# A threshold attention with two feed-forward layers: converted weights kept in memory, the conversion in wide operations on VectorE

## The chip, the core and the metric

One core of one Trainium2 chip. The metric is the device time of one execution in microseconds (us). Before the change three runs took 1331.09, 1331.42 and 1332.36 us; the median is 1331.42.

The engines in the profile: PE (TensorE, matmuls), PEld (its weight loads), DVE (VectorE), ACT (ScalarE), POOL (GpSimd), SP (SyncE, which here issues nearly all transfers on one queue, in program order).

## The reference

The inputs q, k, v have the shape (4, 8, 576, 64): 4 batches, 8 heads, 576 positions, 64 channels. The weights are 64-bit floating-point numbers, the other inputs 32-bit.

```python
scores = q @ k.T / sqrt(64)
keep   = scores >= rowmax(scores) - tau
attn   = softmax over the kept scores
x      = (attn @ v) -> 2304 tokens x 512
h      = sigmoid(x @ w_gate) * (x @ w_val)       # 512 -> 1536
x      = h @ w_out                               # 1536 -> 512
h2     = x @ w2_in                               # 512 -> 2048
g      = h2 if h2 >= 1, 0 if h2 <= -1, else (h2 + 1)**2 / 4
out    = g @ w2_out                              # 2048 -> 512
```

## The kernel before

The kernel sees a weight as a pair of 32-bit words and does no 64-bit arithmetic: each block of 512 columns (128 rows of a layer's weight block) is converted to 32 bit in parts. ScalarE takes the high word and scales it (`convert_a`, L139); VectorE clamps it (L153), shifts it left by three bits (L156), puts the sign in (L159), masks out the power of two (L164), multiplies that by the scaled low word (L169, two operations of 256 columns), and the two parts are added (L175, on GpSimd or VectorE). These are six kinds of operation, 512 columns each.

For precision every matmul operand is split into a rounded high part and the rest. A weight block becomes `ih`/`il` (for the first product) and `oh`/`ol` (for the second): ScalarE writes the high part (L191), the difference is a subtraction (L193, GpSimd). The hidden activations are split in the same way into `hh` (ScalarE, L707) and `hl` (GpSimd, L708). Each product is then three matmuls: high by high, high by low, low by high.

The work has three stages. Attention runs first (the function `attention`, up to about 400 us); in its background the first six blocks are converted into `keep0`. Then `ffn` runs layer 1 and layer 2. A layer goes over the 2304 tokens in three passes of 768 (`NPASS`), and a pass goes over the hidden features in blocks of 128: 12 steps a pass in layer 1, 16 in layer 2. The steps are numbered through here: layer 1 is steps 0 to 11, 12 to 23 and 24 to 35; layer 2 has 48 steps.

In a step of layer 1 TensorE computes, for each half of 384 tokens (n = 0, 1), the gate and the value (`up`, L654 to L656, 12 matmuls each) and then the second product of the step before (`down`, L744). The gate goes through a sigmoid on ScalarE (L692), VectorE multiplies it by the value (L696). The value lies in one PSUM buffer, so TensorE can begin the value of the next half only when VectorE has done this product. In a step of layer 2 VectorE clamps (L700), ScalarE squares (L703) and VectorE takes a maximum (L704).

All converted weights of a layer stay on the chip, in `keep0` and `w32`: layer 1 converts its remaining 30 blocks in the steps of its first pass (three a step, `parts_of`, L783), and in its last pass it converts the 32 blocks of layer 2 over them. The passes between convert nothing. The function `convert` (L658) asks for the raw words of the block three places ahead (`load_w`, L106: two transfers of 256 KB).

The order is written out by hand: each engine executes its instructions in the order in which the code calls them, and a call waits for its operands. At the end of a pass the next pass's tokens are split (`split_xs`, L638: four pieces on ScalarE and four subtractions on VectorE, L646, for each half). The row sums of the last attention pair go through memory: `drain` writes them (rs), `denom` (L461) inverts them and writes dr, `spread` (L469) broadcasts dr into a tile, and `normalise` (L476) multiplies on VectorE.

Of the kernel before, what the change touches and what calls it, by code (L numbers as in the profile page):

```python
# [23 lines left out]
def f32(ap):  # L24

    return ap.bitcast(F32)
# [3 lines left out]
def kernel(  # L30
# [37 lines left out]
    stage = ctx.enter_context(pool("stage", 6))  # L68
    raw = ctx.enter_context(pool("raw", 2))
    zero = ctx.enter_context(pool("zero", 1, space=DRAM))  # L70
    cv = ctx.enter_context(pool("cv", 1))
# [11 lines left out]
    keep0 = const.tile([P, 6 * KD * P], F32, name="keep0")  # L83
# [4 lines left out]
    third = cv.tile([P, 2, KD * P], F32, name="third")  # L88
    raws, wsp, pools, wsp_n = {}, {}, {}, []
    keep, spares = [], []  # L90
# [12 lines left out]
    def nat_tile():  # L103
        return stage.tile([P, S], F32, tag="nat", name="nat")

    def load_w(ph, g):  # L106

        f, i = divmod(g, 3 - ph)
        ins, wo = ((w_gate, w_val), w_out) if ph == 0 else ((w2_in,), w2_out)
        if i < len(ins):  # L110
            src = ins[i][:, 2 * f * P : 2 * (f + 1) * P].rearrange("(k p) f -> p k f", p=P)
        else:
            src = wo[f * P : (f + 1) * P, :].rearrange("p (k f) -> p k f", k=KD)
        hk = KD // 2
        for h in range(2):
            early = ph == 0 and g < 6
            t = raw.tile([P, KD * P], F32, tag="raw", name="raw") if early else nat_tile()[:, : KD * P]
            r = t.bitcast(U32)
            nc.sync.dma_start(
                out=r.rearrange("p (k f) -> p k f", k=hk), in_=src[:, h * hk : (h + 1) * hk]  # L120
            )
            raws[ph, g, h] = r.rearrange("p (f w) -> p f w", w=2)

    def part(g):
        at, o = (keep0, g) if g < 6 else (keep[0], g - 6)
        return at[:, o * KD * P : (o + 1) * KD * P]

    def slot(ph, g):

        n = g % 3  # L130
        if ph == 0 and g < 15:
            n = 2 if g < 6 else (1, 2, 1)[g % 3]
        if n == 2:
            return third[:, 0], third[:, 1]
        if n == 1 and not spares:
            spares.append(raw.tile([P, KD * P], F32, tag="raw", name="raw"))
        return (spares[0] if n else f32(his[0][:, : KD * P])), f32(both[:, n, : KD * P])

    def convert_a(ph, g):  # L139
        c, _ = slot(ph, g)  # L140
        hw = KD * P // 2
        for h in range(2):
            nc.scalar.activation(
                c[:, h * hw : (h + 1) * hw], raws[ph, g, h][:, :, 1].bitcast(F32), AF.Copy, scale=2.0**-112
            )

    def convert_b(ph, gs):


        at = {g: slot(ph, g) for g in gs}  # L150
        hw = KD * P // 2
        for c, a in at.values():
            nc.vector.tensor_scalar(c, c, -DBL_TOP, DBL_TOP, op0=ALU.max, op1=ALU.min)  # L153
            yield
        for c, a in at.values():
            nc.vector.tensor_scalar(a.bitcast(U32), c.bitcast(U32), 3, None, op0=ALU.logical_shift_left)  # L156
            yield
        for c, a in at.values():
            nc.vector.scalar_tensor_tensor(  # L159
                a.bitcast(U32), c.bitcast(U32), 0x80000000, a.bitcast(U32), op0=ALU.bitwise_and, op1=ALU.bitwise_or  # L160
            )
            yield
        for c, a in at.values():
            nc.vector.tensor_scalar(c.bitcast(U32), a.bitcast(U32), 0xFF800000, None, op0=ALU.bitwise_and)  # L164
            yield
        for h in range(2):
            for g, (c, a) in at.items():
                ch = c[:, h * hw : (h + 1) * hw]
                nc.vector.scalar_tensor_tensor(  # L169
                    ch, raws.pop((ph, g, h))[:, :, 0], 2.0**-52, ch, op0=ALU.mult, op1=ALU.mult  # L170
                )
                yield
        for g, (c, a) in at.items():
# [3 lines left out]
    def split_parts(ph, t, f, eng):  # L177
# [10 lines left out]
        for i in range(ni + 1):  # L188
            w = part(f * (ni + 1) + i)
            hi, lo = (oh, ol) if i == ni else (x[:, i].rearrange("p k f -> p (k f)") for x in (ih, il))  # L190
            nc.scalar.activation(hi, w, AF.Copy)  # L191
            yield
            eng.tensor_tensor(lo, w, f32(hi), op=ALU.subtract)  # L193
            yield

    def attention():
# [9 lines left out]
        qk = sb1("qk", 1)  # L206
        per, vp, pe_, pp, ph, sm, tp, rp = (
# [276 lines left out]
        def background():  # L484

            for g in range(6):
# [3 lines left out]
                convert_a(0, g)  # L490
                yield
                yield from convert_b(0, (g,))
# [47 lines left out]
        first = split_parts(0, 0, 0, nc.vector)  # L540
        for t, i in sched:
# [51 lines left out]
            if on:  # L593
# [18 lines left out]
                if t == N - 2:  # L612
                    for g in range(6, 9):
                        load_w(0, g)
# [16 lines left out]
    def ffn(att):  # L631


        with ExitStack() as st:
# [23 lines left out]
            def convert(ph, gs):  # L658
                run(convert_b(ph, gs))
                for g in gs:  # L660
                    i = fresh.index((ph, g)) + 3
                    if i < len(fresh):
                        load_w(*fresh[i])

            def hidden(ph, t, f, parts, after, nxt):
# [4 lines left out]
                ready = (ph, t, f, 0) in early  # L670
                lone = ph == 0 and t == 0
# [217 lines left out]
```

## Time and profile before

| | |
|---|---|
| runs | 1331.09, 1331.42, 1332.36 us |
| profiled execution | 1331.3 us, of which 1329.5 us is the span of its instructions |
| PE busy | 1230.3 us (93%) |
| DVE busy | 809.5 us (61%) |
| POOL busy | 775.6 us (58%) |
| ACT busy | 605.7 us (46%) |
| mean granted TensorE clock | 0.972 of full speed |
| moved by DMA | 87.66 MB |

The shares are averages over stages that differ. The stages are read one by one: attention up to about 400 us, layer 1's pass with a conversion (406 to 587), its pass without (587 to 740), its last pass, which converts for layer 2 (740 to 922), and layer 2 (922 to the end). A busy time of an engine means that an instruction is being executed or held on it; a matmul's end is modelled.

### The profile page before, as it was taken

To read this page: it belongs to the slowest core of one execution; us is meant where nothing else is said; L and a number is where in the kernel's file an instruction comes from. 1 tells how busy PE (TensorE), PEld (TensorE's weight loads), DVE (VectorE), ACT (ScalarE), POOL (GpSimd) and SP (SyncE) were. 2 spreads that over 40 slices of the span, in tenths; PEclk is the share of its full clock that TensorE was granted. 3 is DMA by queue.
4 is the path that set the end of the run, shared out by engine and by line. 5 is a ranking of instruction groups with operands and counts; after the bars stand their busy time and mean duration, and the time that the engine had idled before them with its cause. 6 is when DMAs were issued, how large, how long until landed. Compare 5 with 4: busy or idle time off the path is not lost.

```text
span 1329.5 us, 18928 instructions
## 1 busy us (share of the span) xinstructions
PE 1230.3 (93%) x6904; PEld 1127.6 (85%) x6904; DVE 809.5 (61%) x1148; ACT 605.7 (46%) x1240; POOL 775.6 (58%) x655
## 2 busy tenths in 40 slices
PE   7998999898988888899999888899999999999998
PEld 7887878787887777789999888789999899989997
DVE  6787987977877999951001999996222422243222
ACT  4666666665772333342223433334333533344333
POOL 6576777776774555555344556555555555555553
PEclk8999998998989999999999998989999999999999
DMA  4646565554212332310000233320000000001001
GB/s 139 156 125 158 123 156 138 130 151 120 70 60 69 101 100 96 95 32 1 0 1 0 64 96 103 114 85 1 1 0 1 19 30 1 0 1 48 0 1 48
DMA packets 61921, 87.66 MB, mean 66 GB/s; under 512 B 10832, under 2 KB 33313, under 8 KB 61828
## 3 DMA queue, kind: packets, MB, share of 16 engines
q1 hardware_dynamic: 61684, 86.46, 23.0%
q8 instruction: 54, 0.88, 0.3%
q14 instruction: 39, 0.32, 0.1%
q10 hardware_dynamic: 144, 0.00, 0.0%
HBM read 54.77 MB, written 4.81 MB: 45 GB/s over the span
## 4 chain that ended last, share of the span: by engine, by line
PE 44%; DVE 21%; issue 3%; DMA 2%; ACT 2%; POOL 0%; DVEq 0%; SPq 0%; ACTq 0%; POOLq 0%
PE w L752 14%; PE pu L654 5%; PE pu L655 5%; PE pu L656 5%; PE w L744 5%; DVE both L159 4%; PE pgv L654 3%; PE pgv L656 3%; PE pgv L655 3%; DVE both L156 2%; DVE third L156 2%; DVE act L696 2%; DVE raw L153 2%; DVE third L159 1%; DVE raw L169 1%
## 5 line engine op out<-in xcount | busy, mean ns | idle before, releaser
L708 POOL TENSOR_TENSOR hl<-act,hh 128x384 fp32r<-128x384 f32 x168 | 175.3, 1043 | 331.4 <-ACT hh L707 320.9
L414 POOL TENSOR_TENSOR plo<-p,phi 128x576 fp32r<-128x576 f32 x144 | 209.0, 1452 | 101.5 <-ACT phi L413 95.1
L654 PE MATMUL pgv<-xflat,ih 128*128 128x384 f32 x560 | 197.8, 353 | 50.2 <-DVE act L696 36.3
L707 ACT ACTIVATE hh<-act 128x384 fp32r<-128x384 f32 x168 | 88.2, 525 | 270.9 <-DVE act L696 209.2
L656 PE MATMUL pgv<-xflat,il 128*128 128x384 f32 x560 | 192.6, 344 | 0.0
L655 PE MATMUL pgv<-xflat,ih 128*128 128x384 f32 x560 | 192.3, 343 | 0.0
L654 PEld LDWEIGHTS pgv<-xflat,ih 128*128 128x128 f32 x560 | 108.5, 194 | 67.6 <-DVE act L696 46.2
L700 DVE TENSOR_SCALAR act<-pu 128x384 f32<-128x384 f32 x96 | 53.5, 557 | 174.7 <-PE pu L656 174.7
L193 POOL TENSOR_TENSOR il<-w,ih 128x512 fp32r<-128x512 f32 x99 | 134.7, 1368 | 7.4 <-ACT ih L191 7.4
L703 ACT ACTIVATE act<-act,half 128x384 f32<-128x384 f32 x96 | 58.5, 610 | 172.7 <-DVE act L700 172.7
L406 DVE SCALAR_TENSOR_TENSOR p<-w,cthr,ex 128x576 f32<-128x576 f32 x144 | 116.4, 808 | 30.3 <-ACT ex L400 28.1
L654 PE MATMUL pu<-xflat,ih 128*128 128x384 f32 x384 | 129.7, 338 | 2.2 <-DVE act L704 2.2
L400 ACT ACTIVATE ex<-w 128x576 f32<-128x576 f32 x144 | 93.6, 650 | 81.4 <-PE w L330 39.4
L655 PE MATMUL pu<-xflat,ih 128*128 128x384 f32 x384 | 129.4, 337 | 0.1
L656 PE MATMUL pu<-xflat,il 128*128 128x384 f32 x384 | 129.2, 336 | 0.0
L696 DVE TENSOR_TENSOR act<-pgv,act 128x384 f32<-128x384 f32 x70 | 38.6, 552 | 133.2 <-PE pgv L656 133.2
L356 DVE TENSOR_REDUCE mx<-w 128x1 f32<-128x576 f32 x144 | 107.6, 748 | 17.0 <-PE w L384 11.1
L752 PE MATMUL w<-oh,hh 128*128 128x512 f32 x288 | 113.0, 393 | 0.0
L752 PE MATMUL w<-oh,hl 128*128 128x512 f32 x288 | 112.8, 392 | 0.0
L752 PE MATMUL w<-ol,hh 128*128 128x512 f32 x288 | 112.8, 392 | 0.0
L704 DVE TENSOR_TENSOR act<-pu,act 128x384 f32<-128x384 f32 x96 | 53.5, 557 | 95.2 <-ACT act L703 95.2
L655 PEld LDWEIGHTS pgv<-xflat,ih 128*128 128x128 f32 x560 | 108.7, 194 | 1.1
(159 smaller groups left out, 3102.3 us busy)
## 6 DMA issues: line engine op xcount, KB each, us to landing
nat<-in_moe_w_out_dram SPq DMA_DIRECT2D x52, 256.0 KB
nat<-in_moe_w_in_dram SPq DMA_DIRECT2D x32, 256.0 KB
k<-hi_k SPq DMA_DIRECT2D x50, 144.0 KB
xflat<-hi_q SPq DMA_DIRECT2D x20, 288.0 KB
nat<-in_moe_w_gate_dram SPq DMA_DIRECT2D x20, 256.0 KB
nat<-in_moe_w_val_dram SPq DMA_DIRECT2D x20, 256.0 KB
nat<-in_v_dram SPq DMA_DIRECT2D x16, 288.0 KB
out_dram<-xall SPq DMA_DIRECT2D x17, 256.0 KB
```

The source lines that it names most:

```text
L193: eng.tensor_tensor(lo, w, f32(hi), op=ALU.subtract)
L356: nc.vector.reduce_max(mxs[p % 2][:, u : u + 1], w[:, :, :HS], axis=AX.XY)
L400: nc.scalar.activation(ex, dt[p, u][:, :, :HS], AF.Exp, scale=float(D) ** -0.5)
L406: nc.vector.scalar_tensor_tensor(pr, w[:, :, :HS], cthr, ex, op0=ALU.is_ge, op1=ALU.mult)
L414: nc.gpsimd.tensor_tensor(lo, pr, f32(hi), op=ALU.subtract)
L654: nc.tensor.matmul(ps, ih[:, i, kk], xh[:, kk, c], start=(kk == 0), stop=False)
L655: nc.tensor.matmul(ps, ih[:, i, kk], xl[:, kk, c], start=False, stop=False)
L656: nc.tensor.matmul(ps, il[:, i, kk], xh[:, kk, c], start=False, stop=(kk == KD - 1))
L707: nc.scalar.activation(hh[:, c], act, AF.Copy)
L708: nc.gpsimd.tensor_tensor(hl_[:, c], act, f32(hh[:, c]), op=ALU.subtract)
L744: nc.tensor.matmul(at(y, a, b), l[:, ds_], r[:, c], start=new and m == 0, stop=last and m == 2, skip_group_check=True,)
L752: nc.tensor.matmul(y[i % 3][:, i // 3], l[:, ts_], r, start=first and m == 0, stop=last and m == 2,)
```

## The change

No weights stay on the chip. A group of blocks is now one step's weights: three blocks (1536 columns) in layer 1, two (1024 columns) in layer 2. The clamp, the shift, the sign, the mask and the addition run once for a whole group; the multiplication by the low words stays one operation for each block, of 512 columns now. The result goes into one of five tiles (`ring`) or one of two (`w2s`), and from there to a tensor in the chip's memory (`saved`). Each step of the later passes fetches its weights from there two steps ahead (`load_step`). The groups of layer 2 are converted from step 10 on, five operations a step, over the second and the third pass of layer 1. In layers 1 and 2 every subtraction and addition that GpSimd had is VectorE's, the subtraction for `il` in one operation of 1024 columns in layer 1. GpSimd has no work there any more; its rows go from 494 to 247 in the whole program. Raw words arrive in transfers of 512 KB instead of 256 KB.

The core of the diff:

```diff
     def load_w(ph, g):
-        hk = KD // 2
-        for h in range(2):
-            early = ph == 0 and g < 6
-            t = raw.tile([P, KD * P], F32, tag="raw", name="raw") if early else nat_tile()[:, : KD * P]
+        early = ph == 0 and g < 6
+        t = (raw if early else pools["words"]).tile([P, 2 * KD * P], F32, tag="raw", name="raw")
+        r = t.bitcast(U32)
+        nc.sync.dma_start(out=r.rearrange("p (k f) -> p k f", k=KD), in_=src)
...
+    def load_step(ph, t, f):
+        w32[ph, t, f] = turn()
+        nc.sync.dma_start(out=w32[ph, t, f][:, : (3 - ph) * KD * P], in_=saved[ph, f])
+
+    def extract(ph, gs, c):
+        n = KD * P
+        for i, g in enumerate(gs):
+            nc.scalar.activation(
+                c[:, i * n : (i + 1) * n], raws[ph, g][:, :, 1].bitcast(F32), AF.Copy, scale=2.0**-112
             )
...
+    def convert(ph, gs, c, a):
+        n = KD * P
+        c, a = c[:, : len(gs) * n], a[:, : len(gs) * n]
+        cu, au = c.bitcast(U32), a.bitcast(U32)
+        nc.vector.tensor_scalar(c, c, -DBL_TOP, DBL_TOP, op0=ALU.max, op1=ALU.min)
+        yield
+        nc.vector.tensor_scalar(au, cu, 3, None, op0=ALU.logical_shift_left)
+        yield
+        nc.vector.scalar_tensor_tensor(au, cu, 0x80000000, au, op0=ALU.bitwise_and, op1=ALU.bitwise_or)
+        yield
+        nc.vector.tensor_scalar(cu, au, 0xFF800000, None, op0=ALU.bitwise_and)
+        yield
+        for i, g in enumerate(gs):
+            ci = c[:, i * n : (i + 1) * n]
             nc.vector.scalar_tensor_tensor(
+                ci, raws.pop((ph, g))[:, :, 0], 2.0**-52, ci, op0=ALU.mult, op1=ALU.mult
             )
             yield
-            eng = nc.vector if g % 3 == 2 else nc.gpsimd
-            eng.tensor_tensor(part(g), a, c, op=ALU.add)
+        nc.vector.tensor_tensor(a, a, c, op=ALU.add)
+        yield
...
+            def conversions():
+                for j, (ph, f, gs) in enumerate(todo):
+                    if j == 0:
+                        extract(ph, gs, highs[0])
+                    dst = turn() if ph == 0 else w2s[j % 2]
+                    if ph == 0:
+                        w32[0, 0, f] = dst
+                    ops = convert(ph, gs, highs[j % 2], dst)
+                    for m, _ in enumerate(ops):
+                        if m == 3 + len(gs):
+                            for g in todo[j + 2][2] if j + 2 < len(todo) else ():
+                                load_w(todo[j + 2][0], g)
+                        if m < 4 + len(gs):
+                            yield
+                    nc.sync.dma_start(out=saved[ph, f], in_=dst[:, : len(gs) * KD * P])
+                    if j + 1 < len(todo):
+                        extract(*todo[j + 1][::2], highs[(j + 1) % 2])
+                    yield
...
-                    nc.gpsimd.tensor_tensor(hl_[:, c], act, f32(hh[:, c]), op=ALU.subtract)
...
+                    run(itertools.islice(sp, 1) if n == 0 else itertools.islice(work, 1))
+                    nc.vector.tensor_tensor(hl_[:, c], act, f32(hh[:, c]), op=ALU.subtract)
+                    run(sp)
                     if n == 0 and nxt and nxt[2] == 0:
                         xs = split_xs(*nxt[:2], HT, T)
                         run(split_xs(*nxt[:2], 0, HT))
+                    run(itertools.islice(work, 2) if n == 0 else work)
                 run(xs)
...
+            todo = [(0, f, range(3 * f, 3 * f + 3)) for f in range(2, NF[0])]
+            todo += [(1, f, range(2 * f, 2 * f + 2)) for f in range(NF[1])]
...
                 if free:
+                    pools["words"] = sb("words", 6)
+                    for _, _, gs in todo[:2]:
+                        for g in gs:
+                            load_w(0, g)
...
+            for f in range(2):
+                nc.sync.dma_start(out=saved[0, f], in_=w32[0, 0, f])
...
             for s in range(len(order)):
                 nxt = order[s + 1] if s + 1 < len(order) else None
-                hidden(*order[s], parts_of(s), parts_of(s + 1), nxt)
+                t = order[s][:2]
+                ops = 8 if t == (0, 0) else 5
+                if s + 2 < len(order) and order[s + 2][:2] > (0, 0):
+                    load_step(*order[s + 2])
+                hidden(*order[s], nxt, itertools.islice(conv, ops))
```

How the change moves VectorE's instructions in a step of layer 1's first pass is shown by two pieces of its order. Before, from one product L696 of step 1 to the next, with the conversions of two blocks between them (`third`, `raw`, `both`: the working tiles; `nat`: the raw words; `w`: the kept weights):

```order
L696 TENSOR_TENSOR act<-pgv,act 128x384
L153 TENSOR_SCALAR third<-third 128x512
L156 TENSOR_SCALAR third<-third 128x512
L159 SCALAR_TENSOR_TENSOR third<-third 128x512
L164 TENSOR_SCALAR third<-third 128x512
L169 SCALAR_TENSOR_TENSOR third<-nat,third 128x256 x2
L153 TENSOR_SCALAR raw<-raw 128x512
L156 TENSOR_SCALAR both<-raw 128x512
L159 SCALAR_TENSOR_TENSOR both<-raw,both 128x512
L164 TENSOR_SCALAR raw<-both 128x512
L169 SCALAR_TENSOR_TENSOR raw<-nat,raw 128x256 x2
L175 TENSOR_TENSOR w_4793<-both,raw 128x512
```

Now, the whole of step 2 on VectorE (line numbers of the changed kernel; L689 is the product, L702 `hl`, L183 `il` and `ol`; `high` and `w` are the working tile and the converted weights):

```order
L689 TENSOR_TENSOR act<-pgv,act 128x384
L183 TENSOR_TENSOR il<-w_3_4804,ih 128x1024
L702 TENSOR_TENSOR hl<-act,hh 128x384
L183 TENSOR_TENSOR ol<-w_3_4804,oh 128x512
L147 TENSOR_SCALAR high_4801<-high_4801 128x1536
L149 TENSOR_SCALAR w_4_4805<-high_4801 128x1536
L689 TENSOR_TENSOR act<-pgv,act 128x384
L151 SCALAR_TENSOR_TENSOR w_4_4805<-high_4801,w_4_4805 128x1536
L702 TENSOR_TENSOR hl<-act,hh 128x384
L153 TENSOR_SCALAR high_4801<-w_4_4805 128x1536
L157 SCALAR_TENSOR_TENSOR high_4801<-raw,high_4801 128x512 x3
L161 TENSOR_TENSOR w_4_4805<-w_4_4805,high_4801 128x1536
```

The four subtractions that were GpSimd's stand among VectorE's instructions now, the conversion is spread over both halves of the step, and what the next step splits (`w_4_4805`) is written by the step's last instruction.

The transfers on SP's queue at the end of attention, before (`rs`, `dr` and `both` are the last pair's row sums on their way; `nat` receives raw words):

```order
L473 DMA rb<-dr 128x1x576
L459 DMA rs<-hi_q 64x1x9
L459 DMA rs<-sums 64x1x9
L119 DMA nat<-in_moe_w_gate_dram 128x2x256 x2
L466 DMA dr<-rs 128x9
L473 DMA both<-dr 128x1x576
```

And now (L121 `load_w`, L801 and L663 the stores of converted weights, L450 `drain`, L457 `denom`, L464 `spread`):

```order
L464 DMA rb<-dr 128x1x576
L450 DMA rs<-hi_q 64x1x9
L121 DMA raw<-in_moe_w_gate_dram 128x4x256
L121 DMA raw<-in_moe_w_val_dram 128x4x256
L121 DMA raw<-in_moe_w_out_dram 128x1024
...
L450 DMA rs<-sums 64x1x9
L801 DMA saved_0_89<-w_0_82 128x1536
L801 DMA saved_1_90<-w_1_83 128x1536
...
L663 DMA saved_2_91<-w_2_4803 128x1536
L457 DMA dr<-rs 128x9
L464 DMA both<-dr 128x1x576
```

Six transfers of raw words stand ahead of the last row sums, and two stores, three more transfers of raw words and a third store ahead of the row sums' way back to the chip. In code order the third of those stores and `denom` follow step 0's whole conversion.

## Rows read from the trace of the kernel before

**Rows 1.** Windows: busy time of each engine by stage; the first row names the columns.

```profile
core 0: us, PE busy (x) PEld busy (x) DVE busy (x) ACT busy (x) POOL busy (x), PEclk, DMA share, GB/s
0.00:400.00 400.00, 356.89 (x2316) 326.51 (x2317) 321.95 (x424) 260.35 (x522) 281.09 (x246) 0.94 0.49 127
...
406.00:587.00 181.00, 152.24 (x820) 135.36 (x820) 165.93 (x227) 63.74 (x149) 102.39 (x77) 1.00 0.28 89
587.00:740.00 153.00, 152.83 (x875) 146.19 (x873) 25.31 (x44) 49.02 (x103) 70.02 (x61) 1.00 0.00 1
740.00:922.00 182.00, 161.70 (x851) 151.70 (x852) 169.22 (x233) 66.29 (x153) 106.47 (x81) 0.93 0.26 84
922.00:1329.50 407.50, 401.60 (x2019) 363.31 (x2017) 125.19 (x221) 166.33 (x314) 214.22 (x190) 1.00 0.03 12
```

**Rows 2.** Timeline of VectorE (start us, us, instruction): steps 0, 12, 24; layer 2.

```profile
406.25 0.56 DVE L696 TENSOR_TENSOR act<-w,act 128x384 f32<-128x384 f32 x1
...
586.68 0.56 DVE L696 TENSOR_TENSOR act<-pgv,act 128x384 f32<-128x384 f32 x1 [2.38 <-PE pgv L656]
...
739.30 0.55 DVE L696 TENSOR_TENSOR act<-pgv,act 128x384 f32<-128x384 f32 x1
...
921.75 0.56 DVE L704 TENSOR_TENSOR act<-pu,act 128x384 f32<-128x384 f32 x1 [0.69 <-ACT act L703]
```

**Rows 3.** Timeline of VectorE inside step 1, one conversion.

```profile
418.54 0.41 DVE L153 TENSOR_SCALAR raw<-raw 128x512 f32<-128x512 f32 x1
418.99 1.39 DVE L156 TENSOR_SCALAR both<-raw 128x512 uint32<-128x512 uint32 x1
420.42 0.69 DVE L159 SCALAR_TENSOR_TENSOR both<-raw,both 128x512 uint32<-128x512 uint32 x1
...
422.56 0.76 DVE L169 SCALAR_TENSOR_TENSOR raw<-nat,raw 128x256 f32<-128x256 uint32 x2
423.36 0.69 DVE L175 TENSOR_TENSOR w<-both,raw 128x512 f32<-128x512 f32 x1
```

**Rows 4.** Timeline of GpSimd (POOL), the instruction beside them.

```profile
418.70 1.40 POOL L175 TENSOR_TENSOR w<-third 128x512 f32<-128x512 f32 x1 [0.70 <-DVE third L169]
```

**Rows 5.** Timeline of VectorE: first products of steps 13 and 23.

```profile
599.25 0.56 DVE L696 TENSOR_TENSOR act<-pgv,act 128x384 f32<-128x384 f32 x1 [3.45 <-PE pgv L656]
...
725.16 0.56 DVE L696 TENSOR_TENSOR act<-pgv,act 128x384 f32<-128x384 f32 x1 [7.87 <-PE pgv L656]
```

**Rows 6.** Instructions of L646: durations min/median/max, first and last start.

```profile
L646 DVE TENSOR_TENSOR xflat<-xall,xflat x44: 541/548/1652, 354.9 to 1190.7; 128x384 fp32r<-128x384 f32 x40, 128x768 fp32r<-128x768 f32 x4
```

**Rows 7.** Timeline of VectorE: other widths, alone.

```profile
17.79 0.45 DVE L273 CAST hi_k<-nat 128x576 fp32r<-128x576 f32 x1
...
425.04 0.76 DVE L480 TENSOR_TENSOR xall<-hi_q,both 128x576 f32<-128x576 f32 x1 [0.52 <-DMA both<-dr]
```

**Rows 8.** Timeline of ScalarE (ACT): two widths.

```profile
379.18 0.84 ACT L644 ACTIVATE xflat<-xall 128x768 fp32r<-128x768 f32 x1
...
415.35 0.62 ACT L191 ACTIVATE ih<-w 128x512 fp32r<-128x512 f32 x1
```

**Rows 9.** Chain of waits into the layers: start, us, what.

```profile
396.14 7.84 DMA rs<-hi_q
...
413.52 2.80 DMA dr<-rs
...
416.34 8.68 DMA both<-dr
```

**Rows 10.** Windows of 1 us: the last two columns are DMA share and GB/s.

```profile
401.00:402.00 1.00, 1.00 (x9) 1.00 (x8) 0.00 (x0) 0.00 (x0) 0.00 (x0) 1.00 0.13 51
...
414.00:415.00 1.00, 1.00 (x7) 1.00 (x7) 0.94 (x2) 0.74 (x3) 0.22 (x1) 1.00 0.99 333
...
1063.00:1064.00 1.00, 1.00 (x8) 1.00 (x7) 0.13 (x1) 0.17 (x1) 0.13 (x1) 1.00 1.02 391
```

**Rows 11.** Timeline of VectorE at a layer-2 pass end.

```profile
1049.50 3.85 DVE L646 TENSOR_TENSOR xflat<-xall,xflat 128x384 fp32r<-128x384 f32 x4 [2.11 <-ACT xflat L644]
```

More of the change, by code (lines that the diff above doesn't have):

```diff
@@ L86 @@
     both = const.tile([P, 2, S], F32R, name="both")
-    third = cv.tile([P, 2, KD * P], F32, name="third")
-    raws, wsp, pools, wsp_n = {}, {}, {}, []
-    keep, spares = [], []
+    raws, wsp, pools, wsp_n, highs, stages = {}, {}, {}, [], {}, []
+    w32 = {(0, 0, 0): ring[0], (0, 0, 1): ring[1]}
+    saved = {
+        (ph, f): scratch.tile([P, (3 - ph) * KD * P], F32, name=f"saved{ph}_{f}")
+        for ph in range(2) for f in range(NF[ph])
+    }
     wides = [ps_w.tile([P, 2, 512], F32, name=f"w{i}") for i in range(3)]
@@ L124, in part @@
[L124 to L137, printed above, removed]
@@ L187, in split_parts @@
         wsp[ph, t, f] = (ih, il, oh, ol)
-        for i in range(ni + 1):
-            w = part(f * (ni + 1) + i)
-            hi, lo = (oh, ol) if i == ni else (x[:, i].rearrange("p k f -> p (k f)") for x in (ih, il))
+        n = KD * P
+        fh, fl = (x.rearrange("p i k f -> p (i k f)") for x in (ih, il))
+        steps = [(0, ni)] if whole else [(i, i + 1) for i in range(ni)]
+        at = [(fh[:, i * n : j * n], fl[:, i * n : j * n], i, j) for i, j in steps] + [(oh, ol, ni, ni + 1)]
+        for hi, lo, i, j in at:
+            w = w32[ph, t, f][:, i * n : j * n]
             nc.scalar.activation(hi, w, AF.Copy)
             yield
-            eng.tensor_tensor(lo, w, f32(hi), op=ALU.subtract)
+            nc.vector.tensor_tensor(lo, w, f32(hi), op=ALU.subtract)
             yield
@@ L206, in attention @@
         qk = sb1("qk", 1)
+        stages.append(sb1("stage", 6))
         per, vp, pe_, pp, ph, sm, tp, rp = (
@@ L656, in up, with hidden @@
                     nc.tensor.matmul(ps, il[:, i, kk], xh[:, kk, c], start=False, stop=(kk == KD - 1))
[L658 to L665, printed above, removed]
+            def conversions():
[16 more added lines that the diff above has]
+                    yield
+            def hidden(ph, t, f, nxt, work):
                 hh = hs.tile([P, T], F32R, tag="hh", name="hh")
                 hl_ = hs.tile([P, T], F32R, tag="hl", name="hl")
-                ready = (ph, t, f, 0) in early
-                lone = ph == 0 and t == 0
-                if len(parts) > 2 or parts and not lone:
-                    for p in parts[1:2]:
-                        convert_a(*p)
-                    convert(parts[0][0], [parts[0][1]])
-                    parts = parts[1:]
-                if nxt and nxt not in wsp:
-                    sp = split_parts(*nxt, nc.gpsimd)
-                else:
-                    sp = iter(())
+                sp = split_parts(*nxt) if nxt and nxt not in wsp else iter(())
                 xs = iter(())
@@ L693, in hidden @@
                             up(0, t, f, n, 1, pv)
-                        for p in () if ready else parts[1:] if n == 0 else after[:1]:
-                            convert_a(*p)
+                        if n == 0:
+                            run(itertools.islice(sp, 1))
                         nc.vector.tensor_tensor(act, pv, act, op=ALU.mult)
@@ L720, in hidden @@
                         run(split_xs(*nxt[:2], 0, HT))
+                    run(itertools.islice(work, 2) if n == 0 else work)
                 run(xs)
-                if ready:
-                    for p in parts + after[:1]:
-                        convert_a(*p)
-                    convert(ph, [g for _, g in parts])
-                run(sp)
                 hts[ph, t, f] = (hh, hl_)
@@ L804, in ffn @@
             more = first_up()
[L805 removed]
+            second = split_parts(0, 0, 1, False)
             for step, free in att:
```

84 lines of the change are left out of this document (19 added, 65 removed).

## The prediction, made before the changed kernel was run

> **What bounds the kernel now.** First the windows by stage [rows 1]. In layer 1's first pass VectorE is occupied 165.9 of 181 us and TensorE 152.2; in the second pass, which converts nothing, VectorE falls to 25.3 of 153 and TensorE fills it (152.8); in the third, VectorE is at 169.2 of 182 again. In layer 2 TensorE has 401.6 of 407.5. So TensorE bounds the second pass and layer 2, VectorE the two passes that convert. The starts of VectorE's first products give their lengths [rows 2]: 406.25 to 586.68 is 180.4 us, to 739.30 another 152.6, to layer 2's first maximum at 921.75 another 182.5. TensorE's own pace is read where nothing disturbs it: ten steps take 725.16 - 599.25 = 125.91 us, 12.59 a step [rows 5]; twelve are 151.1.
>
> Next, why VectorE needs so long [rows 3]: two operations of one kind and size, 0.41 us and 1.39 us. Beside the long one GpSimd ran from 418.70 to 420.10 [rows 4], and it ended only 0.28 us later, less than a free one takes. So it did not run slowly, it was held until GpSimd let go. GpSimd has 102 us of work in that pass [rows 1], and the change takes all of it away.
>
> **A conversion step after the change, on VectorE.** Steps 0 to 9 convert three blocks each. Free durations by width:
> - product and `hl`, 384 columns: 0.55 [rows 2, 6]; four of them, 2.20
> - `ol`, 512 columns: 0.69 [rows 3]
> - two-input operations of 1024 and 1536 columns are not in the trace. From 0.55 at 384, 0.69 at 512, 0.76 at 576 [rows 3, 6, 7] one column costs 1.1 ns: 1.25 for `il`, 1.79 each for sign and addition, 4.83 together
> - clamp, shift, mask at 1536: 0.41 at 512 and 0.45 at 576 [rows 3, 7] give about 0.53 ns a column, 0.95; in proportion to the width it would be 1.23. I take 0.95, three times: 2.85
> - multiplication by low words, 512 columns: like other two-input operations, 0.69; the pair of 256 takes 0.76 [rows 3]. Three: 2.07.
>
> The sum is 12.64. One wait is new: the step's first split on ScalarE (1024 columns, 1.06 from 0.62 at 512 and 0.84 at 768 [rows 8]) reads what VectorE's last instruction of the step before wrote, so `il` starts some 1.15 after that; the product in between hides 0.5, leaving 0.6. Behind the waiting `il` stand both `hl`, `ol` and the conversion; TensorE does not wait for them. On the other side independent neighbours overlap by some 0.07 (in rows 3 two of 0.41 take 0.76), about nine places: -0.6. So 12.7, just above TensorE's 12.59. The low end is 12.59; the high end 13.3 without overlap, plus 3 x 0.28 and 2 x 0.28 if widths cost in proportion: 14.7.
>
> [...]
>
> **The way into layer 1.** The first product stays at 406.25: it waits for row sums that land at 403.98 [rows 9], and the transfers ahead of them on SP are the same. Behind them now stand six loads. The broadcast ahead of both keeps a share of 0.13 busy, 2 of 16 engines [rows 10], until about 404, so those engines' part of the loads starts then: 1.57 MB at 333 GB/s [rows 10] is 4.7 us, landing about 410 with completion. Step 0: extraction ends 410.6, clamp and shift 412.5, product, sign, `hl`, mask, three multiplications, addition 420.2 (before, step 1's product came 6.7 us after step 0's; this is 14), and `denom` 420.6. Step 1 lasts 12.7, to 433.3. Then `normalise` needs the last row sums: behind 2.36 MB of loads and a store (7.1 us from 417.5, so to about 425 to 426) `dr` lands 2.8 later and the broadcast 8.7 after that [rows 9], about 437: a wait of 4, plus 0.76. I put step 2's product at 437.3. Between -4 (no wait) and +5.
>
> **The sum.** Eight steps of 12.7 lead to step 10 at 538.9, one of 12.6 to step 11 at 551.5. Step 11 has the splits of the next pass on VectorE too: 2.2 + 1.94 for the step's own, 8 x 0.55 for the token splits, eight operations of two-block groups (1.25 + 1.25 + 4 x 0.68 + 2 x 0.69), together 15.1; 14.5 with overlap. So step 12 comes at 566.0, not 586.68: -20.7 (bounds -26 and +4: 0.1 less a step and no wait; 2 more a step and the wait doubled). The second pass has five operations a step, about 4.2 us beside 4.1 of the step's own, hidden under 12.59; its end has the token splits too (4.1 + 4.4 + 4.2 is 12.7, with waits for ScalarE +0.7): 151.8 against 152.6, -0.8. The third pass likewise: 151.5 against 182.5, -31.0 (bounds -31.4 and -26). Fetches cost nothing as long as a transfer lands within a step: 786 KB at 333 GB/s [rows 10] take 2.4 us, beside loads and stores of at most 4 us in a step of 12.6; if the cover goes, see the second rival. Layer 2: VectorE has 125 of 407 us [rows 1], and each step gets 2.5 us more (`il` and `ol` 0.69 each, two `hl` of 0.55) in 407.5 / 48 = 8.49; at the two pass ends three subtractions (1.9) come before the token splits, which in turn lose GpSimd's contention (3.85 for four [rows 11], 2.2 free): +1 with the faster last `hl` taken off (-1 to +4). Attention: four additions move from GpSimd to VectorE, 0.69 free to 2.1 held each, 2.8 to 8.4; VectorE is occupied 322 of 400 there [rows 1] and waits often, so +1 (-2 to +6).
>
> -20.7 - 0.8 - 31.0 + 1 + 1 = -50.5. The profiled execution took 1331.3 us (span 1329.5 and 1.8 around it), 0.1 below the runs' median, which needs no correction. The forecast is 1281.
>
> **Rivals.**
> - *VectorE stays the bound* with 14.7 a step: wide operations cost in proportion, no overlap. Ten steps are 20 us longer, 1301. For it: no row has these widths, and 12.7 is only 0.1 above TensorE. Against: three widths each lie on a line with a large constant. The other passes hide it.
> - *Fetches become the bound, slower than before.* Each of 72 steps reads weights that SP fetched during the step before. If a fetch ran as slowly as the broadcast in rows 10, 51 GB/s, then 786 KB would take 15.4 us in steps of 12.59 and 524 KB 10.3 in steps of 8.49: 24 x 2.8 + 47 x 1.8 = +152, 1433. It eats the whole gain below some 58 GB/s, where (24 x 786 + 48 x 524) KB over the rate equal 24 x 12.59 + 48 x 8.49 + 50. For it: that broadcast too reads memory written by the kernel, on the same queue. Against: transfers of 128 rows reach a share of 0.99 and 1.02 [rows 10]. [...]
> - *The holding was not GpSimd's*, so the change doesn't free VectorE: operations of one input stay at three times 1.39 for 1536 columns. A step takes 22.3, ten steps +96, and the two-block groups reach 12.8 a step, +5: 1382. Against it the rows where both kinds stand side by side.
>
> **How the numbers follow.** The likeliest course has 0.76 (its own range 1268 to 1294: -4 to +5 at the entry, -1 to +6 over the steps, -3 to +4 at pass ends, -2 to +6 in attention, seldom all at once). VectorE as the bound has 0.15, late fetches 0.03, holding without GpSimd 0.03, a course without a measurable difference 0.03. The range 1266 to 1303 takes in the first two. About 0.2% (2.7 us) is what a measurement of this kernel can tell from no change. Faster is 0.76 + 0.15, so 0.91; same 0.03; slower 0.06.
>
> **What would show it.** Right: 1.0 us or less for the clamp at 1536 columns and about 1.8 for the addition; first products 12.6 to 12.9 apart in steps 2 to 9 and 12.6 in both later passes; TensorE busy as in layer 1's second pass throughout; a wait of a few us at `normalise`. Wrong: fetches that ScalarE's split waits for; the entry later than 410; conversion steps above 13.5; pass ends that cost more than 3 us each.

## The result and the profile after

The changed kernel took 1275.7 us in the median of four runs (1273.4 to 1278.9), the kernel before 1331.3 beside it: a ratio of 0.959 (95% interval 0.956 to 0.962). The forecast was 1281, with a range of 1266 to 1303. The profiled execution took 1278.9 us, its span 1277.1: 52.4 less than the span before.

The windows of the changed kernel by stage, to be laid beside [rows 1]; the last row is one conversion step:

```profile
core 0: us, PE busy (x) PEld busy (x) DVE busy (x) ACT busy (x) POOL busy (x), PEclk, DMA share, GB/s
409.00:567.00 158.00, 150.57 (x824) 143.45 (x825) 140.69 (x178) 65.53 (x115) 0.00 (x0) 0.96 0.57 192
567.00:718.00 151.00, 150.77 (x860) 143.89 (x859) 98.56 (x146) 55.38 (x100) 0.00 (x0) 1.00 0.44 158
718.00:868.50 150.50, 150.50 (x861) 143.95 (x860) 80.39 (x122) 51.05 (x93) 0.00 (x0) 1.00 0.31 111
868.50:1277.00 408.50, 404.66 (x2021) 363.93 (x2019) 229.38 (x411) 171.13 (x314) 0.00 (x0) 1.00 0.20 66
465.00:477.60 12.60, 12.60 (x74) 12.07 (x73) 11.81 (x14) 5.40 (x10) 0.00 (x0) 1.00 0.58 193
```

TensorE is now busy without a gap in layer 1's second and third pass and all but 7.4 us of the first. GpSimd has nothing: the two pages count 655 of its instructions before and 243 now, all in attention. In layer 1 the DMA queues carry 111 to 193 GB/s where they carried 1 to 89, and the only wait for them is that of `normalise`, below. VectorE's first products (the answer to [rows 2]) give the lengths:

```profile
409.39 0.56 DVE L689 TENSOR_TENSOR act<-w,act 128x384 f32<-128x384 f32 x1
...
477.62 0.56 DVE L689 TENSOR_TENSOR act<-pgv,act 128x384 f32<-128x384 f32 x1 [0.58 <-PE pgv L645]
```

Steps 12 and 24 begin at 567.03 and 717.94 and layer 2's first maximum at 868.49, so the three passes take 157.6, 150.9 and 150.6 us (180.4, 152.6 and 182.5 before), and layer 2 408.6 to the end (407.8). In a conversion step the product at 477.62 has waited 0.58 us for TensorE: the bound has changed hands. The wide operations of that step on VectorE, to be laid beside [rows 3]:

```profile
467.91 0.95 DVE L147 TENSOR_SCALAR high<-high 128x1536 f32<-128x1536 f32 x1
...
470.23 1.75 DVE L151 SCALAR_TENSOR_TENSOR w<-high,w 128x1536 uint32<-128x1536 uint32 x1
...
473.36 1.90 DVE L157 SCALAR_TENSOR_TENSOR high<-raw,high 128x512 f32<-128x512 uint32 x3
475.29 1.76 DVE L161 TENSOR_TENSOR w<-w,high 128x1536 f32<-128x1536 f32 x1
```

No operation of this step is held any more: 0.95 us for 1536 columns where one of 512 had taken 1.39.

The only places in layer 1 at which TensorE still starves are at the entry: 2.46 us before 417.36, 1.05 before 422.23 and 3.92 before 438.98. Timeline of VectorE and then of TensorE (PE) around step 2:

```profile
407.24 0.75 DVE L447 COPY hi_q<-aw 64x576 f32<-64x576 f32 x1 [5.70 <-DMA rs<-hi_q]
...
437.70 0.76 DVE L471 TENSOR_TENSOR xall<-hi_q,both 128x576 f32<-128x576 f32 x1 [3.80 <-DMA both<-dr]
438.38 0.55 DVE L689 TENSOR_TENSOR act<-pgv,act 128x384 f32<-128x384 f32 x1
```

```profile
438.98 0.69 PE L643 MATMUL pgv<-xflat,ih 128*128 128x384 f32 x1 [3.92 <-DVE act L689]
439.47 0.52 PE L644 MATMUL pgv<-xflat,ih 128*128 128x384 f32 x1
439.79 0.52 PE L645 MATMUL pgv<-xflat,il 128*128 128x384 f32 x1
```

`normalise` waits 3.80 us for the broadcast and the product stands behind it in VectorE's order, so TensorE idles 3.92 us. After that its matmuls start 0.32 us apart, not 0.17; the windows show why:

```profile
440.00:444.00 4.00, 4.00 (x13) 3.81 (x13) 3.67 (x7) 0.50 (x3) 0.00 (x0) 0.50 0.17 67
444.00:448.00 4.00, 4.00 (x24) 3.50 (x23) 3.97 (x5) 2.12 (x4) 0.00 (x0) 0.94 0.00 0
```

The granted clock is 0.50 in these four microseconds after the idle stretch, and 0.94 in the next four. So step 1 lasts 16.71 us and step 2 14.36, together 5.9 more than two steps of 12.6, around a wait of 3.8 us.

### The profile page after: what moved, and what is told of

The parts are those of the page before. It is cut to its first block, busy times and chain, and to the rows that moved or that the text cites. A ratio compares the mean times of both kernels' runs of the same rounds, so it can differ in the third digit from the quotient of the medians.

```text
span 1277.1 us, 18415 instructions
## 1 busy us (share of the span) xinstructions
PE 1220.7 (96%) x6904; PEld 1126.1 (88%) x6904; DVE 877.0 (69%) x1278; ACT 602.8 (47%) x1138; POOL 275.4 (22%) x243
## 4 chain that ended last, share of the span: by engine, by line
PE 63%; DVE 3%; DMA 2%; issue 1%; ACT 1%; POOLq 0%; POOL 0%; SPq 0%; DVEq 0%; ACTq 0%
PE w L734 15%; PE w L726 11%; PE pgv L643 7%; PE pgv L645 7%; PE pgv L644 7%; PE pu L645 5%; PE pu L643 5%; PE pu L644 5%; DMA both<-dr 1%; DMA rs<-t 1%; DMA dr<-rs 1%; DVE high L157 0%; DVE xflat L635 0%; DVE w L161 0%; DVE p L397 0%
## 5 line engine op out<-in xcount | busy, mean ns | idle before, releaser
L643 PE MATMUL pgv<-xflat,ih 128*128 128x384 f32 x560 | 190.9, 341 | 10.0 <-DVE act L689 5.0
L644 PE MATMUL pgv<-xflat,ih 128*128 128x384 f32 x560 | 190.1, 339 | 0.0
L696 ACT ACTIVATE act<-act,half 128x384 f32<-128x384 f32 x96 | 59.2, 617 | 169.1 <-DVE act L693 169.1
L702 DVE TENSOR_TENSOR hl<-act,hh 128x384 fp32r<-128x384 f32 x168 | 93.5, 557 | 61.9 <-ACT hh L700 61.9
L689 DVE TENSOR_TENSOR act<-pgv,act 128x384 f32<-128x384 f32 x70 | 38.9, 555 | 123.5 <-PE pgv L645 121.8
L643 PEld LDWEIGHTS pgv<-xflat,ih 128*128 128x128 f32 x560 | 106.8, 191 | 13.0 <-DVE act L689 5.6
L644 PEld LDWEIGHTS pgv<-xflat,ih 128*128 128x128 f32 x560 | 106.8, 191 | 1.6
L645 PEld LDWEIGHTS pgv<-xflat,il 128*128 128x128 f32 x560 | 106.6, 190 | 0.0
L420 PE MATMUL aw<-phi,v 128*65 128x288 f32 (+1 forms) x320 | 100.2, 313 | 1.3 <-DVE sums L447 0.6
```

Of the source, the lines that this page charges most:

```text
L420: nc.tensor.matmul(a[: D + 1, :HS], a1, hi[:, s], start=first, stop=False)
L643: nc.tensor.matmul(ps, ih[:, i, kk], xh[:, kk, c], start=(kk == 0), stop=False)
L644: nc.tensor.matmul(ps, ih[:, i, kk], xl[:, kk, c], start=False, stop=False)
L645: nc.tensor.matmul(ps, il[:, i, kk], xh[:, kk, c], start=False, stop=(kk == KD - 1))
L702: nc.vector.tensor_tensor(hl_[:, c], act, f32(hh[:, c]), op=ALU.subtract)
```

## The experiments

All stand on the changed kernel. Ratios are to the kernel before, run beside them.

**Narrow operations.** The group operations are cut into 512 columns:

```diff
-        nc.vector.tensor_scalar(c, c, -DBL_TOP, DBL_TOP, op0=ALU.max, op1=ALU.min)
+        cuts = [slice(i * n, i * n + n) for i in range(len(gs))]
+        for s in cuts:
+            nc.vector.tensor_scalar(c[:, s], c[:, s], -DBL_TOP, DBL_TOP, op0=ALU.max, op1=ALU.min)
...
```

The shift, the sign, the mask and the addition are cut in the same way.

> The changed kernel, but its clamps, shifts, sign, mask and addition operations are cut into 512 columns again (VectorE still does all of it). Theory (the gain has two halves: nothing holds VectorE any more, and wide operations pay their fixed part once): 512 columns cost 0.41 against 0.95/3 for the clamp, shift and mask (+0.28 each per step) and 0.69 against 1.76/3 for the sign operation and the addition (+0.31 each), +1.5 us a step of conversion. VectorE's 12.0 us of work become 13.5 and with its waits on the scalar engine some 13.8 against TensorE's 12.59, so ten steps cost 12 us: 1288 us (1281 to 1294); passes 2 and 3 keep their length. Rival 1 (the width is the whole gain): first pass as before, 1300 us or more. Rival 2 (width is worth nothing, only GpSimd's absence counts): 1276 us.

Measured: 1278.5 us, ratio 0.963 (0.959 to 0.966), not to be told from the changed kernel. The passes, and the steps from step 4 on, have the same lengths to 0.1 us. Timeline of VectorE in a conversion step of this kernel, and the window of the step before it:

```profile
481.75 1.09 DVE L149 TENSOR_SCALAR high<-high 128x512 f32<-128x512 f32 x3
...
484.23 1.89 DVE L155 SCALAR_TENSOR_TENSOR w<-high,w 128x512 uint32<-128x512 uint32 x3
...
491.73 0.56 DVE L695 TENSOR_TENSOR act<-pgv,act 128x384 f32<-128x384 f32 x1 [0.53 <-ACT ih L187]
```

```profile
466.50:479.10 12.60, 12.60 (x74) 12.07 (x73) 12.14 (x25) 5.29 (x9) 0.00 (x0) 1.00 0.56 185
```

Three operations in a row overlap: 1.09 against 0.95, 1.89 against 1.75. Each of the five groups costs 0.14 more, not 0.28 to 0.31, and some of that is given back, since the first narrow operation of a group starts before the last of the group ahead has ended (the next group comes 1.01 us after the clamp at 481.75, against 0.98). VectorE is busy 12.14 of the 12.60 us, against 11.81; it idles 0.53 us before the product at 491.73 (the split named in that line ends just then, but the product does not read it) and TensorE not at all, so it is still under TensorE's pace. My theory's second half falls: the width is worth 0.3 us of busy time a step and nothing of the time, as the second rival said.

**GpSimd back, and both back.** GpSimd gets `hl`, `il`, `ol` and two thirds of the addition again (in layer 2's groups the whole addition), with wide operations and then with narrow ones:

```diff
+    def split_parts(ph, t, f, whole=True, eng=nc.vector):
...
+            eng.tensor_tensor(lo, w, f32(hi), op=ALU.subtract)
...
+                sp = split_parts(*nxt, eng=nc.gpsimd) if nxt and nxt not in wsp else iter(())
...
-                    nc.vector.tensor_tensor(hl_[:, c], act, f32(hh[:, c]), op=ALU.subtract)
+                    nc.gpsimd.tensor_tensor(hl_[:, c], act, f32(hh[:, c]), op=ALU.subtract)
...
-        nc.vector.tensor_tensor(a, a, c, op=ALU.add)
+        for i in range(len(gs)):
+            eng = nc.gpsimd if i < 2 and len(gs) > 1 else nc.vector
+            s = slice(i * n, i * n + n)
+            eng.tensor_tensor(a[:, s], a[:, s], c[:, s], op=ALU.add)
```

> The changed kernel with wide conversion operations, but GpSimd has again what it had before: hl, il, ol in layers 1 and 2 and two thirds of the addition. VectorE's own work falls by 4.1 us a step to 7.9 us. Theory (GpSimd's operations hold VectorE's clamps, shifts and masks until they end, as 0.41 us became 1.39 before): GpSimd runs some 8.6 us of a step, each of the three wide operations is held by 1 to 2 us, and the products in the next part wait behind them: a conversion step of 13 to 14.5 us, 1290 us (1280 to 1310), with 0.95 us operations shown at 1.5 us or more. Rival (no holding; the gain is fewer and wider operations and the work's new places): VectorE has the less to do and TensorE sets the steps as in the changed kernel, 1276 us or less.

> The changed kernel with both undone: conversion operations of 512 columns, and GpSimd has hl, il, ol and two thirds of the addition again; the memory round trip and the spreading of the second layer's conversion over two passes stay. Theory: the first pass is back at about the 14.7 us a step of before (nine held operations a step), +20 to 25 us against the changed kernel; passes 2 and 3 stay near TensorE's bound since a step there has only five operations: 1300 us (1290 to 1312). Rival 1 (the memory round trip alone made the gain): 1276 us. Rival 2 (the engine and the width made all of it, the spreading nothing): as before the change, 1331 us.

Measured: 1299.1 us wide (ratio 0.978, 0.974 to 0.982) and 1302.7 narrow (0.982, 0.978 to 0.986). A conversion step takes 14.30 and 15.29 us in place of 12.6 (before the change 16.1, not the 14.7 that my expectation names), the first pass 173.8 and 176.6; the second takes 155.2 and 153.1, the third 151.3 and 152.5. VectorE and GpSimd in the same stretch of the wide kernel:

```profile
481.87 3.05 DVE L149 TENSOR_SCALAR w<-high 128x1536 uint32<-128x1536 uint32 x1
...
489.42 3.69 DVE L157 SCALAR_TENSOR_TENSOR high<-raw,high 128x512 f32<-128x512 uint32 x3
493.14 1.66 DVE L164 TENSOR_TENSOR w<-w,high 128x512 f32<-128x512 f32 x1
```

```profile
481.12 2.99 POOL L186 TENSOR_TENSOR il<-w,ih 128x1024 fp32r<-128x1024 f32 x1 [1.17 <-ACT ih L184]
484.07 1.73 POOL L705 TENSOR_TENSOR hl<-act,hh 128x384 fp32r<-128x384 f32 x1
```

The shift takes 3.05 us beside `il` on GpSimd, 0.96 alone. VectorE has 4.1 us less to do and is occupied 14.16 of the step's 14.30 us, against 11.81. Where GpSimd disturbs, width counts after all (1.0 us a conversion step); fewer operations to hold would explain it, but no run separates that. With both undone 27 us of the 55 are gone between the medians, 26 by the stages of the profile and 31 by the ratios. What stays, 0.8 us of a conversion step and above all the third pass at 152.5, is neither the engine nor the width of these operations; the subtraction of 1024 columns, the multiplications of 512, the new places in the order and the memory round trip are still the changed kernel's.

**GpSimd beside an unchanged VectorE.** GpSimd repeats the subtractions into a tile that nobody reads, while VectorE keeps all its work (the copies of `il` and `ol` run in layer 2 as well, which the text below leaves out):

```diff
             nc.vector.tensor_tensor(lo, w, f32(hi), op=ALU.subtract)
+            if whole:
+                nc.gpsimd.tensor_tensor(ghost[0][:, : (j - i) * n], w, f32(hi), op=ALU.subtract)
...
+                    if ph == 0:
+                        nc.gpsimd.tensor_tensor(ghost[0][:, :HT], act, f32(hh[:, c]), op=ALU.subtract)
```

> The changed kernel with GpSimd repeating in layer 1 the subtractions il, ol and hl that VectorE makes, into a tile that nobody reads: VectorE's work and everybody's inputs are unchanged, GpSimd is busy some 5.8 us of every step. Theory (holding): the clamp and the shift behind il and ol run into GpSimd's 2.5 and 1.3 us operations, the mask into hl's 1.0 us: 2 to 3 us a conversion step, VectorE at 14 to 15 us against TensorE's 12.59, the first pass 15 to 25 us longer, passes 2 and 3 as they are: 1296 us (1286 to 1306). Rival (the engines do not disturb one another): 1276 us.

Measured: 1344.0 us, ratio 1.012 (1.009 to 1.016): some 1% slower than before the change. Conversion steps take 17.4 us, the first pass 206.4 (+49), the others and layer 2 +7, +2 and +10. VectorE, GpSimd beside it, and the window of the step:

```profile
491.23 1.23 DVE L184 TENSOR_TENSOR il<-w,ih 128x1024 fp32r<-128x1024 f32 x1 [0.66 <-ACT ih L182]
492.37 2.74 DVE L705 TENSOR_TENSOR hl<-act,hh 128x384 fp32r<-128x384 f32 x1
495.03 1.50 DVE L184 TENSOR_TENSOR ol<-w,oh 128x512 fp32r<-128x512 f32 x1
496.46 2.05 DVE L148 TENSOR_SCALAR high<-high 128x1536 f32<-128x1536 f32 x1
```

```profile
491.34 3.36 POOL L186 TENSOR_TENSOR ghost<-w,ih 128x1024 fp32r<-128x1024 f32 x1 [6.24 <-ACT ih L182]
494.77 1.21 POOL L707 TENSOR_TENSOR ghost<-act,hh 128x384 fp32r<-128x384 f32 x1
496.06 1.63 POOL L186 TENSOR_TENSOR ghost<-w,oh 128x512 fp32r<-128x512 f32 x1
```

```profile
490.00:507.40 17.40, 14.46 (x72) 13.59 (x72) 16.64 (x15) 4.96 (x9) 8.03 (x4) 0.90 0.43 138
```

The mechanism is shown: VectorE's work and inputs are the same, and 8 us of GpSimd's time in a step cost 4.8. GpSimd's copies could also have cost time by keeping buffers from being written again; but VectorE's own operations take 16.64 us of the step instead of 11.81, and these 4.8 are the whole of it. The size was underestimated because I had the clamp, shift and mask alone in the sum, and GpSimd at 5.8 us a step in place of 8.0. Subtractions are held as well: `hl` 2.74 for 0.55, `ol` 1.50 for 0.68, the clamp 2.05 for 0.95. They end 0.41, 0.55 and 0.82 us after GpSimd's operation beside them, each 0.13 or 0.14 less than it takes alone: the same picture as the 0.28 for 0.41 from which the prediction read the holding.

**Layer 2's conversion in the last pass.** The middle pass converts nothing. Steps 10 and 11 keep their eight operations each, as in the changed kernel, so 16 of layer 2's 112 operations still run in the first pass and 96 in the last:

```diff
-                ops = 8 if t == (0, 0) else 5
+                ops = {(0, 0): 8, (0, 2): 10}.get(t, 0)
```

> The changed kernel, but the second layer's conversion stays in the last pass of the first layer as before (10 operations a step there, none in the middle pass). Theory (GpSimd's operations, not the crowding into one pass, made the last pass 182 us before): the wide operations of 1024 columns cost about 0.66 us (three), 1.2 us (two) and 0.63 us (two), 5.6 us a part, 16 parts in 12 steps are 7.5 us a step; with 4.1 us of products and splits VectorE works 11.6 us of TensorE's 12.59, plus some 1.3 us of waits for the extraction where one part follows the other within a step: the last pass 151 to 160 us and 1280 us (1273 to 1288). Rival (the spreading is what took 31 us out of the last pass): the last pass at 170 us or more, 1297 us or more.

Measured: 1280.9 us, ratio 0.963 (0.961 to 0.966). The third pass takes 155.6 us, 5 more, and all of it in its first two steps (15.75 and 14.52): the copies out of the accumulators of the pass before stand behind ten conversion operations on VectorE, the first at 726.22, 12 us after the step's product. The other steps have TensorE's 12.6. VectorE is busy 129.0 of the pass's 155.6 us. So in the third pass two things suffice, either without the other: without GpSimd, one pass holds six sevenths of the conversion; spread over two passes, GpSimd and narrow operations together cost 2 us (152.5). That both are needed to make the 182 us of before is inferred: no run puts GpSimd back into the unspread pass.

**No fetches in layer 2's passes 2 and 3** (stale weights).

```diff
-        nc.sync.dma_start(out=w32[ph, t, f][:, : (3 - ph) * KD * P], in_=saved[ph, f])
+        if ph == 0 or t == 0:
+            nc.sync.dma_start(out=w32[ph, t, f][:, : (3 - ph) * KD * P], in_=saved[ph, f])
```

> The changed kernel without the 32 fetches of the second layer's passes 2 and 3 (512 KB each; those passes compute with stale weights, so that part of the output is not the reference's). Theory (the fetches are hidden): the same time, 1275 us, nothing waits for a fetch. Side question, why the second layer's step is 8.41 us against 8.34 us before the change, all of it in the 18 matmuls of 512 columns (0.2338 us apart against 0.2294): if the fetches' writes do it, passes 2 and 3 fall back to 8.34 us a step and the time to 1273 us; if it is something else (where the tiles lie, who makes the splits), they stay at 8.41 us. Rival to the theory (the fetches cost time): more than 4 us shorter.

Measured: 1276.9 us, ratio 0.960 (0.958 to 0.963). These fetches are hidden; and the steps stay at 8.41 us, so they are not what spaces the matmuls.

**Late normalisation, and a tile for the row.**

```diff
-                if s == 0:
+                if s == 1:
                     denom(NP - 1)
-                if s == 1:
+                if s == 5:
                     normalise(NP - 1)
```

```diff
+                if p == NP - 1:
+                    row = f32(both[:1, 1]).rearrange("p (a b) -> p a b", a=2)
+                    todo = [(tt[p][:D], a[:D, :, :HS]), (row, a[D : D + 1, :, :HS])]
```

> The changed kernel, with the reciprocal of the last head pair's denominators behind step 1 instead of step 0, and its normalisation behind step 5 instead of step 1 (its result is needed at the third pass alone). Theory (VectorE's 3.8 us wait there stops the products behind it, TensorE runs dry, and then runs the next matmuls at half the granted clock): the intervals 16.7 and 14.4 us between the products of steps 1, 2 and 3 become about 12.6 to 13 us, 5 us less: 1271 us (1268 to 1274). Rival (the conversion of step 1 sets that interval, and the wait lies beside it): 16 us and 1276 us.

> As the kernel with the late normalisation, and the last head pair's first row of denominators is copied to a tile of its own, so that the second head's copy out of the accumulators does not wait for the transfer of that row (5.70 us at 407.24 in the changed kernel, which TensorE's first product of step 0 waits for with 2.3 us). Theory: some 2 us less than with the late normalisation alone, 1269 us (1265 to 1273). Rival: the transfer was over when the accumulators were ready, or something else (the loads, the scalar engine) is next: as the late normalisation alone, within 1 us.

Measured: 1271.2 us (ratio 0.955, 0.952 to 0.959), and with both edits 1270.0 (0.955, 0.952 to 0.958). With the late normalisation the intervals after step 0 are 13.00, 12.62, 12.63: the wait, the idle stretch of 3.92 us and step 2's slow matmuls are gone together, 5.4 us between the first products of steps 0 and 4 (55.65 to 50.21). Steps 0 and 1 of the changed kernel have shorter idle stretches too, 2.46 and 1.05 us, which this edit does not aim at; after the first of them the granted clock is 0.50 for 2.9 us (417.36 to 420.30). The second edit takes away VectorE's wait for the row, and its copy now waits for TensorE alone:

```profile
402.75 0.75 DVE L450 COPY hi_q<-aw 64x576 f32<-64x576 f32 x1 [2.49 <-PE aw L422]
```

Step 0's product then comes 3.4 us earlier after the last `il` of attention, but step 0 lasts 13.62 us in place of 11.96: its clamp now waits 2.14 us for the extraction (1.14 with the late normalisation alone), which itself waits 0.72 us for raw words. In the two profiled executions 3.1 us remain from that `il` (398.16 and 398.39) to layer 2's last step (1254.12 and 1257.41); between the medians it is 1.1 us, which can't be told from nothing.

**Where the tiles lie.** Left to explain were layer 2's steps of 8.41 us against 8.34. GpSimd's return did not change them (8.41), nor did the fetches. An unused tile moves `hh` and `hl` by 32 bytes, or by 64:

```diff
+            kp.tile([P, 8], F32, name="pad")
             conv = conversions()
```

The control has 16 in place of 8. The addresses in the two texts below come from the layout of the kernels; no trace shows them.

> The changed kernel with one unused tile of 32 bytes a partition behind the others, which moves hh and hl (and the conversion's tiles) from addresses that are a multiple of 32 bytes but not of 64 to multiples of 64, as they were before the change (hh at 178112 in place of 178144; before the change at 154752). No instruction changes. Theory (where hh and hl lie makes the second layer's step 8.41 us instead of 8.34): the 18 matmuls of 512 columns, whose stationary operand they are, fall from 0.2338 to 0.2294 us apart, the step to 8.34 us, 48 steps give 3.5 us: 0.997 of the changed kernel's time. Rival (something else): 0.2338 us and 8.41 us, the same time.

> The control to the 32-byte tile: 64 bytes instead, so that hh and hl move by 64 bytes and stay at an odd multiple of 32 (178080). Theory (the alignment): 0.2338 us and 8.41 us as in the changed kernel. Rival (any move of the tiles does it): 0.2294 us and 8.34 us.

Measured, with 32 bytes: 1273.3 us (0.956, 0.953 to 0.958; the changed kernel in that group 0.960). The starts of the first down-matmul and of the up-matmul behind the 18 of them, in two steps of layer 2 in this kernel:

```profile
891.51 0.40 PE L734 MATMUL w<-oh,hh 128*128 128x512 f32 x1
...
895.71 0.34 PE L643 MATMUL pu<-xflat,ih 128*128 128x384 f32 x1
...
899.88 0.39 PE L734 MATMUL w<-oh,hh 128*128 128x512 f32 x1
...
904.01 0.35 PE L643 MATMUL pu<-xflat,ih 128*128 128x384 f32 x1
```

They take 4.20 and 4.13 us, in the changed kernel 4.19 to 4.21 in every step, and before 4.14 in the mean (4.10 to 4.20): one step in three reaches that, the others gain 0.01. `oh` and `ol` rotate over three places, `hh` and `hl` over two. Before the change the 18 matmuls take 4.10 to 4.20 us in a cycle that repeats every six steps, as the places of the two pairs do together. Layer 1's steps fall from 12.62 to 12.55 as well. From step 4 to layer 2's last step it is 795.2 us, against 798.7 in the changed kernel; with 64 bytes 797.1, its layer 2 steps at 8.40 (one execution, 1271.5 us). So addresses alone move matmul spacing by up to 1.9% (4.21 to 4.13) with no instruction changed. That a multiple of 64 decides is at most a part of it: which address of which operand counts stays open.

**All together**, and the changed kernel again beside it:

> Late normalisation, the row of denominators in a tile of its own, and the 32-byte tile, together. Theory: 5.5 us (entry) and 3.5 us (alignment) less than the changed kernel: 0.993 of its time, about 1266 us. Rival (the alignment is nothing): 1270 us.

> The changed kernel once more, unedited, beside the others of this group, as the base of their comparison. Expected: 1276 us (1272 to 1280), 8.41 us a step in the second layer.

Measured: 1266.5 us (1262.2 to 1268.0), ratio 0.950 (0.948 to 0.952); the changed kernel 1278.3, ratio 0.960 (0.958 to 0.962). This version beats both; it takes 0.991 of the changed kernel's time, where 0.993 was expected.

## Why the prediction was right

- *VectorE was held by GpSimd and is freed by the change.* Right, and shown from both sides: with GpSimd back 1299 us, with GpSimd only repeating work 1344.
- *A conversion step of 12.7 us, VectorE's sum just above TensorE.* The step is 12.6, but TensorE's. VectorE is busy 11.8. The widths came out at 0.95 (predicted 0.95) and 1.75 (1.79), `il` at 1.22 (1.25); the multiplications take 0.63 each (0.69). The 0.95 is nearer than its rows could promise: 0.04 us over 64 columns is 0.6 ns a column, not 0.53, and would give 1.05. The wait of 0.6 for the split does not show here, because VectorE waits for TensorE anyway and the split ends meanwhile. It is there where VectorE lags behind, as it does in steps 3 and 4 of the kernel with both edits at the entry:

```profile
443.49 0.55 DVE L692 TENSOR_TENSOR act<-pgv,act 128x384 f32<-128x384 f32 x1
444.70 1.23 DVE L183 TENSOR_TENSOR il<-w,ih 128x1024 fp32r<-128x1024 f32 x1 [0.67 <-ACT ih L181]
...
455.98 0.55 DVE L692 TENSOR_TENSOR act<-pgv,act 128x384 f32<-128x384 f32 x1
```

There VectorE waits for nothing but the split, and a step is 12.49 us. That is VectorE's own pace: the prediction had it 0.2 too long, and it lies only 0.1 below TensorE's 12.6. Which engine is the bound came out the other way round, at almost no cost in time. The rival's 14.7 was far off: narrow operations alone add 0.3 us of busy time and don't reach TensorE's pace.
- *The entry.* Step 0 was put at 406.25 and came at 409.39. But in other executions of kernels with the same attention it came between 401.3 and 410.8, the unedited one again at 405.6, so nothing can be read from 3 us. Extraction ended at 412.3 (410.6), the addition at 421.4 (420.2), and the wait at `normalise` was 3.8 us (4): step 2 at 438.38 against 437.3. The road there was right too: `dr`, issued at 421.89, landed 6.17 later behind the queue, at 428.06 (427.8 to 428.8 by the prediction's terms), and the broadcast took 9.60 (8.7). What I missed is the half clock after it, 1.8 us in step 2.
- *Steps to 12.* Step 10 at 540.7 (538.9), step 11 13.71 us (14.5), step 12 at 567.03 (566.0).
- *Passes 2 and 3.* 150.9 and 150.6 us (151.8 and 151.5): the pass ends cost nothing. The prediction put the third pass's 31 us into one term, with the operations spread and free at once; the runs show that either was nearly enough.
- *Layer 2 +1.* +0.9, but not by that road, and so by luck: the steps cost 0.07 more each (+3.5, in part the tiles' addresses), the two pass ends gave 3.4 us back, so that first and last maximum lie 395.2 us apart in both kernels, and the 0.9 stand behind the last maximum (13.4 us to the end, 12.6 before).
- *Fetches hidden.* Right: without two thirds of layer 2's the time is the same, and in layer 1 the trace has no wait for one. A fetch of 512 KB is over after some 2.2 us of layer 2's step of 8.41, where the 51 GB/s of the second rival would have needed 10.3:

```profile
897.70:899.90 2.20, 2.20 (x13) 2.02 (x12) 1.12 (x2) 0.76 (x2) 0.00 (x0) 1.00 0.78 238
899.90:906.10 6.20, 6.20 (x33) 5.56 (x32) 3.40 (x6) 2.56 (x5) 0.00 (x0) 1.00 0.00 0
```

Against the sum of -50.5, the span fell by 52.4: -2.1 in the first pass, -0.9 and -1.0 in the others and -0.1 in layer 2, +2.1 in attention. The last lies within the spread of the first product's start, so an agreement to 2 us is in part luck. The rest of the 5 us to the median is the profiled execution, the longest of the four.

## What to carry to other kernels

Where VectorE and GpSimd work side by side, count GpSimd's busy time against VectorE before counting what it takes off it: 8 us of it cost 4.8 us a step here, and giving it 4.1 us of VectorE's work made the step 1.7 us longer. Make operations wider for the engine that sets the pace (1.0 us a step here with GpSimd beside it); when another does, it buys slack (0.3 us). An operation whose result is needed late belongs late in its engine's order, all the more when its wait lets TensorE run dry, because that was paid again in clock here (0.50 for some 5.5 us, which made step 2 1.8 us longer).

## What the runs showed of the hardware

- Holding goes both ways and includes two-input operations: GpSimd's `hl` took 1.73 us beside VectorE's conversion (1.0 alone), and VectorE's 0.55 us became 2.74. The three held operations beside GpSimd's copies ended 0.41, 0.55 and 0.82 us after them, each 0.13 or 0.14 less than it takes alone.
- TensorE idle for 3.92 us came back at a granted clock of 0.50 and kept it for some 5.5 us (438.98 to 444.5).
- The spacing of 512-column matmuls was 0.230 us before and 0.234 after, in the mean of a step and at a granted clock of 1.00 in both, and a shift of the tiles by 32 bytes alone brought it back in one step of three.
